# A planned instruction order replaced by another: new ranks and new engine choices for 1,088 steps of an RWKV6-plus-MLP kernel

## The chip, the cores and the metric

The kernel runs on one core of a Trainium2 chip. The metric is the time of one execution on the device in microseconds (us); smaller is better. The core has five engines that run side by side and wait for each other through semaphores: TensorE (PE; matmuls and, listed apart as PEld, their weight loads), VectorE (DVE), ScalarE (ACT), GpSimd (POOL) and SyncE (SP, which here issues nearly all DMA transfers). Each engine takes its instructions strictly in the order in which they were recorded. So an instruction that waits holds back everything recorded behind it on its engine, and the order in which independent work is recorded matters.

## The reference: what is computed

```python
def _attn_ref(r, k, v, w, u):                      # (4, 8, 768, 48) each, u (8, 48)
    for t in range(S):
        cur = np.einsum('bhd,bhe->bhde', u[None] * kt, vt)
        y[:, :, t] = np.einsum('bhd,bhde->bhe', rt, state + cur)
        state = wt[:, :, :, None] * state + np.einsum('bhd,bhe->bhde', kt, vt)

def _moe_ref(x, w_in, w_out):                      # x (3072, 384), w_in (384, 2048), w_out (2048, 384)
    h = x @ w_in
    g = np.maximum(0.01 * h, h)
    return g @ w_out
```

A linear-attention recurrence with per-channel decay w runs over 768 time steps for 4 batches of 8 heads; its output, 3072 rows of 384, goes through two dense layers with a leaky ReLU between them.

## The kernel before, in words

**Tiling.** The recurrence is cut into chunks of 128 time steps, 6 per batch, 24 in all, numbered in the order in which they are worked. The first two chunks of two batches are done as "pairs" (pair 0 is chunks 0 and 1, pair 1 chunks 2 and 3); chunks 4 to 23 are "singles", some of them merged in twos for their score matmuls. Within a chunk the recurrence is matmuls:

- SP loads w, k, r and v (L553 for pairs, L768 for singles), into a slot of the pool "in", which has ten.
- ScalarE takes the logarithm of w (lw, L567 and L778). TensorE sums it along time (L577, L784, with column totals at L591 and L787). VectorE makes ci (L796), ScalarE exponentials (L610, L810, L814; of the totals, a, L600 and L805), VectorE multiplies them onto r and k (rk, L468).
- rk is transposed to rkT by TensorE (L479, evacuated at L484 by VectorE or L486 by ScalarE) or, for 13 chunks, by a transposing DMA from SP (L831).
- TensorE makes scores (L691, L925), VectorE masks them (m, L703, L855); then TensorE makes the chunk's output from m and the cast v (vb) and from the carried state (L716, L723, L891, L896). The carried state is scaled by GpSimd (sb, L842), v is cast by GpSimd (vb, L518), the chunk's contribution to the state is made by TensorE (L650, L865) and added by VectorE (L880).
- The "bonus" of u: GpSimd multiplies k by u (ru, L498) and by r (L502), VectorE sums (dg, L506), GpSimd multiplies by v (L510; its result is named y in pairs, vs in singles). It is added by TensorE in pairs (L735) and by VectorE in singles (L541).
- The output y is transposed into xT by TensorE (L527, evacuated at L532 by VectorE or L534 by ScalarE) or, for 8 chunks, by DMA (L910).

The two dense layers are worked in 15 blocks of one or two chunks: "up" matmuls (L1087) into a bank of PSUM, the leaky ReLU by ScalarE (g, L1102), "down" matmuls (L1117), a copy to SBUF (o, L1128 or L1130), a store from SP (L1134). The last three blocks use a scheme with seven products instead of eight (sums at L1002, products at L1019, combinations at L1031 to L1040, stores at L1070). The weights w_in and w_out are loaded in parts by SP (L389, L394) and cast by whichever of GpSimd (L411), VectorE (L413) or ScalarE (L415) is chosen. L1159 are filler matmuls on zeros that stand in gaps of the first 24 us, to keep TensorE's clock up.

**What sets the order.** The program first lists 1,090 steps (`step(...)`): for each the engines that may do it with a planned duration on each, a priority number, the steps it depends on and the buffers it takes. Then `Plan.order` plays these through as a list scheduler: at each moment a free engine takes the ready step with the lowest priority number whose buffers are free. The order in which steps come out is the order in which their instructions are recorded, on every engine and in SP's DMA queue; buffers, too, are given out there. Two tables tune it. `RANK` has an offset for a step's priority number, `FORCE` fixes the engine of steps that several could do:

```python
        for i, x in RANK.items():
            plan.steps[i][2] = round(plan.steps[i][2] + x, 3)
        for i, e in FORCE.items():
            plan.steps[i][0] = {e: plan.steps[i][0][e]}
        order = plan.order(pools)
```

The recording loop behind it calls each step's function in that order, and puts filler matmuls ahead of a TensorE step where the plan has a gap.

Of the kernel before, what the change touches and what calls it, by code (L numbers as in the profile page):

```python
# [23 lines left out]
class Plan:  # L24
# [135 lines left out]
STORE = (0.45, 8, 0.9, 0.2)  # L160
TRK = (1.7, 64, 0.9, -0.6)
TY = (0.95, 24, 0.7, -0.6)
RANK = {0: 15.37, 1: 14.4, 2: 3.33, 3: 23.03, 5: 38.76, 6: 12.01, 7: -26.8, 8: -21.87, 9: -21.96, 10: -19.05,
# [63 lines left out]
FORCE = {24: "DVE", 27: "DVE", 30: "ACT", 31: "DVE", 47: "ACT", 59: "ACT", 62: "ACT", 80: "ACT", 86: "DVE",  # L227
    113: "DVE", 115: "ACT", 118: "DVE", 120: "ACT", 122: "ACT", 124: "DVE", 126: "POOL", 128: "ACT", 129:
    "POOL", 135: "POOL", 138: "DVE", 140: "POOL", 143: "ACT", 144: "POOL", 493: "DVE", 501: "ACT", 605: "DVE",
    613: "ACT", 905: "DVE", 911: "DVE", 933: "ACT", 953: "ACT", 967: "ACT", 1003: "ACT", 1031: "ACT", 1076:  # L230
    "ACT", 1081: "ACT"}


@with_exitstack
def kernel(
# [95 lines left out]
    with tc.manual_schedule():  # L331
# [810 lines left out]
        step({"PE": 0.0}, lambda e: None, 1000.0, deps=[up_first[2]], reads=[warm])  # L1142
# [51 lines left out]
```

## Time and profile before

| | |
|---|---|
| median of 3 runs | 181.74 us (180.81 to 182.94) |
| the profiled execution | 180.97 us, of which the span from first to last instruction is 179.3 us |
| TensorE clock granted in it | 0.997 of full speed |
| TensorE busy | 170.3 us of 179.3 |
| VectorE, ScalarE, GpSimd busy | 131.9, 116.5, 103.4 us |
| moved by DMA | 34.43 MB, mean 192 GB/s |

"Busy" is the time in which at least one instruction of the engine ran. The page cuts the span into 40 slices and gives the busy share of each in tenths. The timeline of an engine lists its instructions in order of time, equal neighbours merged: start, duration from the first's start to the last's end, engine, line, operation, tiles; in square brackets the idle time ahead and what ended it. As matmuls are pipelined, the listed end of one may lie behind the start of the next; starts are what is compared here.

### The profile page before, as it was taken

To read this page: it belongs to the slowest core of one execution; us is meant where nothing else is said; L and a number is where in the kernel's file an instruction comes from. 1 tells how busy PE (TensorE), PEld (TensorE's weight loads), DVE (VectorE), ACT (ScalarE), POOL (GpSimd) and SP (SyncE) were. 2 spreads that over 40 slices of the span, in tenths; PEclk is the share of its full clock that TensorE was granted. 3 is DMA by queue.
4 is the path that set the end of the run, shared out by engine and by line. 5 is a ranking of instruction groups with operands and counts; after the bars stand their busy time and mean duration, and the time that the engine had idled before them with its cause. 6 is when DMAs were issued, how large, how long until landed. Compare 5 with 4: busy or idle time off the path is not lost.

```text
span 179.3 us, 5364 instructions
## 1 busy us (share of the span) xinstructions
PE 170.3 (95%) x2102; PEld 133.8 (75%) x2105; DVE 131.9 (74%) x266; ACT 116.5 (65%) x259; POOL 103.4 (58%) x138
## 2 busy tenths in 40 slices
PE   7798899999989999999999999999999999999991
PEld 2555778867868688787688777777778798899991
DVE  7799664189769899459687659499787599777472
ACT  4679868855957688895379775176685487735620
POOL 5998532675697586878468855414996448110000
PEclk9999999999999999999999999999999999999998
DMA  6999999999999899999999999979799996813004
GB/s 150 261 284 317 371 378 358 185 195 201 227 185 203 170 223 143 182 208 184 200 199 194 220 178 229 208 151 140 146 205 140 195 214 139 184 24 115 0 22 154
DMA packets 116716, 34.43 MB, mean 192 GB/s; under 512 B 109138, under 2 KB 115923, under 8 KB 116691
## 3 DMA queue, kind: packets, MB, share of 16 engines
q1 hardware_dynamic: 116688, 34.09, 94.6%
q8 instruction: 16, 0.26, 0.7%
q14 instruction: 10, 0.07, 0.2%
q10 hardware_dynamic: 2, 0.00, 0.0%
HBM read 25.17 MB, written 4.72 MB: 167 GB/s over the span
## 4 chain that ended last, share of the span: by engine, by line
PE 57%; DMA 12%; POOL 8%; issue 7%; SPq 6%; DVE 4%; ACT 4%; DVEq 0%; POOLq 0%; ACTq 0%
PE ps L1087 26%; PE ps L1117 14%; DMA in<-in_v_dram 8%; PE ps L1019 6%; SPq L553 4%; DMA in<-in_k_dram 3%; PE ps L925 2%; POOL ru L498 2%; SPq L389 2%; DMA in<-in_r_dram 2%; ACT g L1102 2%; POOL ru L502 2%; POOL sb L842 1%; DVE o L1040 1%; PE ps L896 1%
## 5 line engine op out<-in xcount | busy, mean ns | idle before, releaser
L1087 PE MATMUL ps<-xT,w_in_b 128*128 128x256 bf16 (+1 forms) x720 | 73.2, 251 | 0.2 <-ACT xT L534 0.2
L1102 ACT ACTIVATE g<-ps 128x512 bf16<-128x512 f32 x96 | 56.5, 595 | 20.7 <-PE ps L1087 15.2
L1087 PEld LDWEIGHTS <-w_in_b 128*128 128x128 bf16 x720 | 57.5, 98 | 9.2 <-issue 0.7
L1117 PE MATMUL ps<-w_out_b,g 128*128 128x384 bf16 x288 | 56.0, 326 | 0.1
L1117 PEld LDWEIGHTS <-g 128*128 128x128 bf16 x288 | 25.7, 97 | 12.3 <-ACT g L1102 0.2
L498 POOL TENSOR_TENSOR ru<-in,ub 128x384 f32<-128x384 f32 x24 | 24.6, 1028 | 11.0 <-DMA in<-in_k_dram 10.8
L468 DVE TENSOR_TENSOR rk<-in,ps 128x384 bf16<-128x384 f32 x48 | 25.0, 549 | 7.4 <-ACT ps L810 4.2
L855 DVE TENSOR_TENSOR m<-ps,maskb 128x512 bf16<-128x512 f32 x40 | 25.4, 684 | 6.1 <-PE ps L925 5.1
L502 POOL TENSOR_TENSOR ru<-ru,in 128x384 f32<-128x384 f32 x24 | 24.3, 1018 | 2.7 <-DMA in<-in_r_dram 2.1
L842 POOL TENSOR_TENSOR sb<-s,a 128x384 bf16<-128x384 f32 x18 | 15.7, 873 | 8.9 <-ACT a L805 8.7
L510 POOL TENSOR_TENSOR vs<-in,dg 128x384 f32<-128x384 f32 x20 | 16.6, 828 | 7.4 <-DVE dg L506 4.9
L518 POOL CAST vb<-in 128x384 bf16<-128x384 f32 x24 | 12.0, 504 | 12.0 <-DMA in<-in_v_dram 12.0
L506 DVE TENSOR_REDUCE dg<-ru 128x8 f32<-128x384 f32 x24 | 13.1, 546 | 2.3 <-POOL ru L502 2.1
L796 DVE TENSOR_TENSOR ci<-ps,lw 128x384 f32<-128x384 f32 x20 | 11.1, 554 | 3.7 <-PE ps L784 1.7
L778 ACT ACTIVATE lw<-in 128x384 bf16<-128x384 f32 x20 | 10.4, 520 | 3.0 <-DMA in<-in_w_dram 3.0
L810 ACT ACTIVATE ps<-ps 128x384 f32<-128x384 f32 x20 | 9.5, 474 | 4.1 <-DVE ci L796 3.8
L541 DVE TENSOR_TENSOR y<-ps,vs 128x384 bf16<-128x384 f32 x20 | 11.1, 554 | 1.4 <-PE ps L896 0.6
L880 DVE TENSOR_TENSOR s<-ps,sb 128x384 f32<-128x384 f32 x14 | 7.7, 552 | 3.9 <-PE ps L865 1.4
L814 ACT ACTIVATE ps<-ci 128x384 f32<-128x384 f32 x20 | 9.8, 488 | 0.6 <-DVE ci L796 0.6
L805 ACT ACTIVATE a<-ps 64x4 f32<-64x4 f32 x36 | 6.0, 167 | 5.6 <-DVE ci L796 3.8
L534 ACT COPY xT<-ps 128x384 bf16<-128x384 bf16 x11 | 5.2, 478 | 6.9 <-PE ps L527 6.9
L1019 PEld LDWEIGHTS <-g 128*128 128x128 bf16 x96 | 8.0, 98 | 0.5 <-ACT g L1102 0.4
(105 smaller groups left out, 222.3 us busy)
## 6 DMA issues: line engine op xcount, KB each, us to landing
out_dram<-o SPq DMA_DIRECT2D x23, 192.0 KB, 3.2
in<-in_w_dram SPq DMA_DIRECT2D x20, 192.0 KB, 4.2
in<-in_k_dram SPq DMA_DIRECT2D x20, 192.0 KB, 4.2
in<-in_r_dram SPq DMA_DIRECT2D x20, 192.0 KB, 4.3
in<-in_v_dram SPq DMA_DIRECT2D x20, 192.0 KB, 4.3
in<-in_moe_w_out_dram SPq DMA_DIRECT2D x4, 768.0 KB, 12.1
in<-in_moe_w_in_dram SPq DMA_DIRECT2D x4, 384.0 KB, 7.0
in<-in_moe_w_in_dram SPq DMA_DIRECT2D x2, 768.0 KB, 9.2
```

Source lines behind the costliest of these rows:

```text
L468: (nc.gpsimd if e == "POOL" else nc.vector).tensor_tensor(out=o, in0=x, in1=i, op=ALU.mult)
L498: lambda e: nc.gpsimd.tensor_tensor(out=ru.t[:], in0=kv(), in1=ubv, op=ALU.mult),
L502: lambda e: nc.gpsimd.tensor_tensor(out=ru.t[:], in0=ru.t[:], in1=rv(), op=ALU.mult),
L506: lambda e: nc.vector.tensor_reduce(out=dg.t[:], in_=ru.t[:], axis=AX.X, op=ALU.add),
L510: lambda e: nc.gpsimd.tensor_tensor(out=vs.t[:], in0=vv(), in1=dg.t[:].unsqueeze(2).to_broadcast([128, H, D]), op=ALU.mult),
L518: {"POOL": 0.56}, lambda e: nc.gpsimd.tensor_copy(out=vb.t[:], in_=vv()),
L842: lambda e: nc.gpsimd.tensor_tensor(out=sb.t[:].rearrange("p g a d -> p (g a) d"), in0=s_in.t[:].rearrange("p g a d -> p (g a) d"), in1=a_ ...
L855: lambda e, par=par: nc.vector.tensor_tensor(out=m.t[:, par, :, :], in0=sc[par].t[:].rearrange("p (g t) -> p g t", g=NP), in1=maskb[:].uns ...
L1019: nc.tensor.matmul(o(), lhsT=x()[:, i, :], rhs=y()[:, i, :], start=fresh, stop=(stop and i == ii[-1]), skip_group_check=True)
L1087: nc.tensor.matmul(hp.t[:, a * N : (a + 1) * N], lhsT=w_in_b[:, t, (j + a) * 128 : (j + a + 1) * 128], rhs=xT[:, t, c0 : c0 + N], start=(a ...
L1102: lambda e, hp=hp, g=g, j=j, J=J, N=N: nc.scalar.activation(out=g.t[:, j : j + J, 0:N], in_=hp.t[:, 0 : J * N].rearrange("p (a n) -> p a n ...
L1117: nc.tensor.matmul(op.t[:, 0:DM], lhsT=g.t[:, j, off : off + 128], rhs=w_out_b[:, j, :], start=(j == 0), stop=(j == NJ - 1))
```

## The change

The change replaces the two tables and nothing else; no function is touched. Below it `RANK` gets offsets for all steps from 0 to 1087 (before: 0 to 144, 492 to 716 and 902 to 1087, with gaps), `FORCE` fixes the engine of 69 steps (before: 36). The new tables come from a search in which every operation of VectorE, ScalarE and GpSimd was lengthened at random. The first lines of each:

```diff
-RANK = {0: 15.37, 1: 14.4, 2: 3.33, 3: 23.03, 5: 38.76, 6: 12.01, 7: -26.8, 8: -21.87, 9: -21.96, 10: -19.05,
-    11: -14.59, 12: 18.77, 13: 18.75, 14: -2.55, 15: 18.27, 16: -16.59, 17: -21.47, 18: -19.49, 19: -20.48,
...
+RANK = {0: -59.43, 1: -52.42, 2: -98.27, 3: -101.28, 4: -69.43, 5: 951.62, 6: -68.29, 7: -162.82, 8: -162.92,
+    9: -101.74, 10: -20.83, 11: -89.42, 12: -137.74, 13: 931.61, 14: -77.73, 15: 931.11, 16: -90.39, 17:
...
-FORCE = {24: "DVE", 27: "DVE", 30: "ACT", 31: "DVE", 47: "ACT", 59: "ACT", 62: "ACT", 80: "ACT", 86: "DVE",
...
+FORCE = {4: "ACT", 24: "DVE", 27: "ACT", 30: "DVE", 33: "ACT", 47: "ACT", 57: "ACT", 59: "ACT", 60: "ACT", 62:
...
```

What comes out, by listing both programs' instructions on each engine:

| engine | steps before | steps after | mean shift in place | largest |
|---|---|---|---|---|
| TensorE | 320 | 320 | 3.2 | 22 |
| VectorE | 248 | 247 | 2.0 | 16 |
| ScalarE | 258 | 258 | 2.4 | 20 |
| GpSimd | 120 | 121 | 2.3 | 12 |
| SP (transfers) | 144 | 144 | 3.2 | 23 |

39 steps change their engine (weight casts, evacuations of rkT and xT, copies of o, two first states). Filler matmuls go from 36 to 41. In the first stage the changes that stand out are these:

- SP's queue: 1st part of w_in ahead of pair 1's k instead of behind it; then, behind pair 1's v, second quarter of w_out, first quarter of w_out, last quarter of w_in, third and fourth quarter of w_out (before: first quarter of w_out, last of w_in, second, fourth, third of w_out).
- GpSimd, pair 1: vb, vb, y, y (before: y, vb, vb, y).
- TensorE: eight groups of L1087 (of 0.65 us or a little more each) stand between pair 1's L735 and the first L1117 (before: five).

Later, SP loads some chunks' k or v ahead of an earlier chunk's r or v: chunk 7's w and k come before chunk 6's r and v; chunk 10's v goes from the 52nd to the 60th place in the queue. GpSimd's L498 for chunk 7 comes before chunk 6's vb, for chunk 10 before chunk 9's L498 and chunk 10's sb, for chunk 12 before the vb and the sb of chunk 11. The order of TensorE's last eleven steps stays as it was. All line numbers of the changed kernel are 73 higher behind the tables (L1087 becomes L1160, and so on).

More of the change, by code (lines that the diff above doesn't have):

```diff
@@ L162 @@
 TY = (0.95, 24, 0.7, -0.6)
-RANK = {0: 15.37, 1: 14.4, 2: 3.33, 3: 23.03, 5: 38.76, 6: 12.01, 7: -26.8, 8: -21.87, 9: -21.96, 10: -19.05,
[63 rows of a table removed]
-FORCE = {24: "DVE", 27: "DVE", 30: "ACT", 31: "DVE", 47: "ACT", 59: "ACT", 62: "ACT", 80: "ACT", 86: "DVE",
[L228 to L231, printed above, removed]
+RANK = {0: -59.43, 1: -52.42, 2: -98.27, 3: -101.28, 4: -69.43, 5: 951.62, 6: -68.29, 7: -162.82, 8: -162.92,
[133 rows of a table added]
+FORCE = {4: "ACT", 24: "DVE", 27: "ACT", 30: "DVE", 33: "ACT", 47: "ACT", 57: "ACT", 59: "ACT", 60: "ACT", 62:
+    "ACT", 80: "ACT", 83: "DVE", 86: "DVE", 89: "ACT", 103: "DVE", 113: "DVE", 115: "DVE", 116: "ACT", 120:
+    "ACT", 122: "POOL", 124: "POOL", 126: "ACT", 128: "ACT", 129: "POOL", 131: "POOL", 132: "ACT", 134: "DVE",
+    135: "POOL", 137: "DVE", 138: "DVE", 141: "POOL", 143: "DVE", 158: "DVE", 160: "ACT", 187: "ACT", 189:
+    "DVE", 198: "ACT", 202: "DVE", 240: "ACT", 262: "DVE", 278: "ACT", 280: "ACT", 309: "DVE", 311: "ACT",
+    325: "DVE", 384: "DVE", 422: "ACT", 436: "DVE", 493: "DVE", 613: "ACT", 737: "ACT", 771: "ACT", 785:
+    "ACT", 799: "ACT", 849: "ACT", 855: "ACT", 877: "DVE", 883: "ACT", 905: "ACT", 933: "ACT", 939: "DVE",
+    953: "ACT", 967: "ACT", 1003: "ACT", 1031: "DVE", 1034: "ACT", 1039: "ACT", 1076: "ACT", 1081: "ACT"}
 @with_exitstack
```

194 rows, old and new, of the table RANK are left out of this document.

## The prediction

> **What bounds the kernel now.** I read the page first, then the windows, then the timeline of TensorE around every hole, then the same stretch on the engine named as the releaser. The page:
>
> ```profile
> PE 170.3 (95%) x2102; PEld 133.8 (75%) x2105; DVE 131.9 (74%) x266; ACT 116.5 (65%) x259; POOL 103.4 (58%) x138
> PE   7798899999989999999999999999999999999991
> PEclk9999999999999999999999999999999999999998
> ```
>
> TensorE is the bound: busy 95%, at full clock (0.997 granted over the span), full in nearly every slice from the sixth to the last but one. A busy matmul may overlap the next, so I measure holes another way: from the start of one group of matmuls to the start of the next, less what the same group takes elsewhere when nothing waits (four L1117 0.65 us, twelve 128-column L1087 0.67, four L479 0.22, eight L1019 0.66). The timeline of TensorE at the largest hole after the start:
>
> ```profile
> 52.46 0.39 PE L479 MATMUL ps<-ident,rk 128*128 128x128 bf16 x4
> 53.45 0.33 PE L865 MATMUL ps<-vb,rk 128*128 128x96 bf16 x4 [0.60 <-POOL vb L518]
> ```
>
> 53.45 - 52.46 - 0.22 = 0.77 us. The same reckoning gives 0.38 at 62.0 (L1087 waits for ScalarE's xT copy, L534), 0.17 and 0.22 at 132, 0.27 at 149 (L1019 waits for the third of three g's in a row), 0.49 at 174.7 (L1019 waits for VectorE, L1040), and 0.26 in three small ones: **2.6 us from 23.6 us on**. Each group of scores (L925) also loses about 0.1 us before and after it (38.58 to 39.33 for four L1117 is 0.75, not 0.65), a dozen times; the change keeps these groups, so that stays.
>
> Before 23.6 us TensorE waits for pair 1 (the second batch's first two chunks). GpSimd's rows there, then TensorE's:
>
> ```profile
> 19.89 0.83 POOL L510 TENSOR_TENSOR y<-in,dg 128x384 bf16<-128x384 f32 x1 [2.53 <-DMA in<-in_v_dram]
> 20.66 0.95 POOL L518 CAST vb<-in 128x384 bf16<-128x384 f32 x2
> 21.57 0.83 POOL L510 TENSOR_TENSOR y<-in,dg 128x384 bf16<-128x384 f32 x1
> ...
> 21.66 0.47 PE L650 MATMUL ps<-vb,rk 64*128 64x96 bf16 x14 [0.23 <-POOL vb L518]
> ```
>
> The v load lands shortly before 19.89, GpSimd does one bonus multiply (y), then the two vb casts, and only then can L650 run: 0.69, 0.40 and 0.38 us of hole between 20.5 and 22.8. At the other end, L1019's last eight matmuls start at 175.16, the last store at 176.40, and the span ends at 179.3.
>
> So: from the L1087 at 23.62 to the end of the matmuls at 175.98 are 152.4 us, 2.6 of them holes. The set of steps left at that point is the same in the new order, so are their durations and the tail. The time can change only through (a) when that point comes, (b) the holes, (c) the tail.
>
> **The change part by part.** No arithmetic is added; all 320 TensorE steps keep their set and move by 3.2 places on average, at most 22. 39 steps change between VectorE, ScalarE and GpSimd (xT copies, rkT evacuations, weight casts, o copies), leaving 247, 258 and 121 steps against 248, 258 and 120: the loads move by under 1 us per engine, and none of the three is above 74%. Filler matmuls (L1159) go from 36 to 41, all ahead of 24 us; they stand where the planner saw gaps, and TensorE has 1.5 us of holes there, more than five of them (0.06 us for 128 columns, 0.22 for 512): nothing.
>
> (a) *The start.* GpSimd now does both vb casts (0.95) ahead of the first y multiply: L650 can start 0.8 us earlier (20.85). The final add of pair 1 (L735) needs both y's, which end at 22.4 as before, so it moves from 23.19 to about 22.5: -0.7. What is late next: chunk 4's first matmul (L784, at 35.36) has the same amount of TensorE work ahead of it and its w load still stands behind all weights in SP's queue. Its ScalarE logarithm ran at 34.56, 0.4 us before its k load (GpSimd waits until 34.93 for that). So most of the 0.7 is waited for again there. Bounds 0 and -0.7; I take **-0.3**.
>
> *Weights.* SP now fetches the second quarter of w_out, then the first, and the last quarter of w_in after both. The transfers landed at 24.99, 27.02, 29.11, 31.19 and 33.35 (rows of L411 and L413 that wait for them), so the one that moves comes 2.1 us later or earlier. The first L1117 needs the first quarter: landed 27.02, cast by 27.85; TensorE gets to it, after three groups of L1087 more than now (0.67 each) at 28.4. Covered by 0.6. The last quarter of w_in, 29.11, is cast by 30.0 and used at 31.0. Covered by 1.0; if the start gains nothing, by 0.7 more each.
>
> One cover is thinner than that. Where a GpSimd and a VectorE cast began together, one was long:
>
> ```profile
> 33.38 1.22 POOL L411 CAST w_out_b<-in 128x768 bf16<-128x768 f32 x1 [1.37 <-DMA in<-in_moe_w_out_dram]
> 33.35 0.56 DVE L413 CAST w_out_b<-in 128x768 bf16<-128x768 f32 x1 [3.68 <-DMA in<-in_moe_w_out_dram]
> ```
>
> against 0.83 alone: +0.39. Before has two such pairs (27.0, 33.4), the new order three. At 27.02 this would leave 0.2 of the 0.6. The Trainium skill (SBUF — State Buffer, section Who interferes with whom) says that such a VectorE copy locks GpSimd out for its whole length; by that the pair would cost 0.56, not 0.39, and the first L1117 would just be covered. The trace has the one cast lengthened, by less than that.
>
> (b) *The holes.* The 0.77 at 52.5: L865 waits for chunk 7's vb. On GpSimd that cast stood behind L498 (ru), which waited until 49.42 for chunk 7's k, and behind vs, sb and the second ru (0.82 + 0.83 + 0.99). Now one ru (1.00) stands between, 1.6 us less, and the k load goes out before chunk 6's r and v and before three stores. The hole goes: **-0.77** (0 if L498 waits longer than now).
> The 0.38 at 62.0: the copy moves from ScalarE (0.48, behind two a's that waited for ci) to VectorE (0.36, where masks and ci are queued): **-0.2**, between 0 and -0.38. Small ones: **-0.1** of 0.26.
> New: at 131 a cumulative sum (L784) follows the L1087 that allows its logarithm after 0.65 us of TensorE work, where it had 1.30; the one that now has 0.82 lost 0.17, so this one 0.17 + 0.17: **+0.3**. The 0.39 at 132 and 0.27 at 149 keep their distances. Three down groups come 1.00 to 1.10 us after the L1087 whose g they need (they had 1.30 to 7). At 149 a distance of 0.92 cost 0.27, so about 1.19 is needed when three g's queue, and 0.92 when none does: 0 to +0.4; **+0.2**.
> The rest: some 300 moves whose cover no row shows. Count of dependencies through another engine with under 0.3 us to spare in TensorE work: 19 before, 16 now; under 1 us: 64 and 74. It is no looser an order. Below by 0, above by as much as this order has, 2.6; nearer the low end, as two thirds of the present holes are priced already: **+0.5**.
>
> (c) *The tail.* One output copy (L1033, 0.35 in VectorE's chain of 173.20 to 175.1) goes to ScalarE, whose own next copy then ends the wait: bounds 0 and -0.35; **-0.1**.
>
> Sum: -0.3 - 0.77 - 0.2 - 0.1 + 0.3 + 0.2 + 0.5 - 0.1 = -0.5 us. The profiled execution took 180.97 (span 179.3 and 1.7 around it): 180.5. Its own time is 0.8 under the median of 181.74; against the median the same sum gives **181.2**.
>
> **Rivals.**
> 1. *As many holes, elsewhere.* The new waits equal those removed; only the start's -0.3 or nothing is left: 181.7. For it: the counts above. Against: the largest hole has a plain cause that is moved.
> 2. *The order has air where the old one had none.* All 2.6 of holes but the 0.39 + 0.27 kept go, with the start's 0.3 and 0.2 of the tail: -2.4, so 179.3. For it: most holes come from a step that was a little late, and that is what lengthening at random punishes. Against: the tight distances counted, and 0.3 at 131.
> 3. *Slower: GpSimd is held by L498.* L498 for chunks 7, 10 and 12 now stands ahead of a vb or sb that is needed sooner. It waited 10.8 us for k in 11 places, 0.98 each, where mostly nothing urgent stood behind. If the k loads land no earlier against GpSimd's place, three such waits reach L865 or the L891 that need vb and sb: +2.9 in place of the +0.5, and the -0.77 gone, which leaves -0.2 of the other terms: +2.7, so 184.4 uncovered; a quarter of it covered gives 183.7. It decides where a k lands over 0.5 us after GpSimd gets to it. Against: SP issues those k loads earlier.
> 4. *That it does nothing* can't be: the orders differ on all five queues.
>
> **How the numbers follow.** Forecast 0.35, rival 1 0.18, rival 2 0.21, rival 3 0.26. A change of under 1% (1.8 us) is about what a measurement here can't tell from none, so forecast and rival 1 are "same": faster 0.21, same 0.53, slower 0.26. The range goes from rival 2 to rival 3, with 0.3 to 0.5 for the bounds of the small terms: 179.0 to 184.2.
>
> **What would show it.** L650 of pair 1 at about 20.9 and chunk 4's L784 still near 35.2; no wait of L865 for vb near 52; a short wait of L784 near 131; the tail 3.3 us after the last matmul. A wait of L865 or L891 for GpSimd over 0.7 us, behind an L498 that waits for k, shows rival 3. I would be wrong if weights land in another rhythm, or if VectorE or ScalarE queues, of which I priced only what made a hole before, hold TensorE.

## The result, and the profile after

Beside each other on one chip the kernel before took 181.38 us (median of 20 executions) and the changed one 180.77 (20). The ratio is **0.9935, with a 95% interval of 0.9911 to 0.9959**, 1.2 us faster, when executions that lie over 1.5% above the fastest of their kernel are left out (five of these twenty of the changed kernel, 182.44 to 184.75, and one of the six of e12 below; with them the two medians are 0.6 us apart). Repeated on two other chips the ratio was 0.9917 [0.9890, 0.9944] and 0.9908 [0.9874, 0.9942], 1.5 and 1.7 us. The forecast said 0.5 us faster, under 1% and so "same": range and class hold, the gain by the ratios is 2.4 to 3.4 times as large. The profiled executions show less of it (180.97 us, span 179.3, against 180.35, span 178.6), since executions of one kernel spread over some 2 us and one profile is one of them.

The changed kernel's page:

```profile
PE 171.6 (96%) x2110; PEld 135.0 (76%) x2110; DVE 130.2 (73%) x265; ACT 116.1 (65%) x259; POOL 104.7 (59%) x139
PE   7898999999999999999999999999999999999992
PEclk9999999999999999999999999999999999999998
```

TensorE still bounds, at full clock. GpSimd's timeline in the start (start, duration, engine, line, tiles; in brackets the idle time ahead and its cause):

```profile
19.68 0.96 POOL L591 CAST vb<-in 128x384 bf16<-128x384 f32 x2 [1.55 <-DMA in<-in_v_dram]
20.60 1.61 POOL L583 TENSOR_TENSOR y<-in,dg 128x384 bf16<-128x384 f32 x2
```

Both vb casts now run ahead of both y's. TensorE's timeline (L723 is L650 of before, L808 is L735, L938 is L865, L552 is L479, L1190 is L1117):

```profile
21.21 0.51 PE L723 MATMUL ps<-vb,rk 64*128 64x96 bf16 x16
...
22.80 0.50 PE L808 MATMUL ps<-y,spread 64*128 64x384 bf16 x4
...
51.86 0.81 PE L1190 MATMUL ps<-w_out_b,g 128*128 128x384 bf16 x4
52.51 0.33 PE L938 MATMUL ps<-vb,rk 128*128 128x96 bf16 x4
52.68 0.39 PE L552 MATMUL ps<-ident,rk 128*128 128x128 bf16 x4
...
65.06 0.62 PE L552 MATMUL ps<-ident,rk 128*128 128x128 bf16 x8 [0.21 <-DVE rk L541]
...
127.61 0.83 PE L1160 MATMUL ps<-xT,w_in_b 128*128 128x128 bf16 x12 [0.32 <-DMA xT<-y]
...
156.18 0.40 PE L998 MATMUL ps<-rkT 48*128 48x128 bf16 x8 [0.25 <-DMA rkT<-rk]
...
174.82 0.82 PE L1092 MATMUL ps<-w_out_b,in 128*128 128x192 bf16 x8 [0.25 <-DVE o L1113]
```

The sums start at 21.21, and the state's matmul at 52 us follows its down group without a gap: the largest hole of before is gone. But there are new ones: transposes that wait for rk (hole 0.37 us, from start to start), up products that wait for xT's transposing DMA (0.48), scores that wait for rkT's (0.41). By the same reckoning as in the prediction, from 23 us on:

| profile | first sum (L784) of chunk 4 | holes 23-54 us | 54-115 | 115-170 | 170- | all | last matmul to end | span |
|---|---|---|---|---|---|---|---|---|
| before | 35.20 | 0.76 | 0.50 | 0.65 | 0.48 | 2.40 | 3.53 | 179.3 |
| before, repeated (e3) | 35.06 | 0.80 | 1.27 | 0.64 | 0.49 | 3.20 | 3.53 | 179.8 |
| after | 34.90 | 0.21 | 0.92 | 0.89 | 0.41 | 2.44 | 3.24 | 178.6 |
| after, repeated (e4) | 34.97 | 0.12 | 0.37 | 1.50 | 0.41 | 2.41 | 3.22 | 178.7 |
| after, third (e12) | 34.66 | 0.90 | 0.34 | 0.31 | 0.42 | 1.97 | 3.22 | 177.7 |

"Last matmul to end" counts from the start of the last matmul in the trace. Means of the two and the three: the start 0.29 earlier (35.13 to 34.84), holes 0.53 less (2.80 to 2.27), the end 0.30 shorter (3.53 to 3.23). That is 1.1 us, close to the difference of the mean spans (1.2, from 179.5 to 178.4) and to what the timed executions give. The first pair of profiles differs by 0.6, near the forecast, but by other pieces than forecast: 0.30 at the start, nothing in the holes, 0.28 at the end. So three pieces had to be tested: the start, the holes, the end.

### The profile page after: what moved, and what is told of

It reads as the page before. It is cut to its first block, busy times and chain, and to the rows that moved or that the text cites. A ratio compares the mean times of both kernels' runs of the same rounds, so it can differ in the third digit from the quotient of the medians.

```text
span 178.6 us, 5383 instructions
## 1 busy us (share of the span) xinstructions
PE 171.6 (96%) x2110; PEld 135.0 (76%) x2110; DVE 130.2 (73%) x265; ACT 116.1 (65%) x259; POOL 104.7 (59%) x139
## 4 chain that ended last, share of the span: by engine, by line
PE 58%; DMA 14%; SPq 11%; DVE 4%; POOL 4%; ACT 4%; issue 3%; POOLq 0%; DVEq 0%
PE ps L1160 23%; PE ps L1190 14%; SPq L841 10%; PE ps L1092 8%; DMA in<-in_k_dram 5%; DMA xT<-y 3%; DMA in<-in_v_dram 3%; DMA rkT<-rk 2%; POOL ru L571 2%; PE ps L998 2%; DMA in<-in_r_dram 2%; PE ps L552 1%; PE ps L969 1%; PE ps L1232 1%; PE ps L964 1%
## 5 line engine op out<-in xcount | busy, mean ns | idle before, releaser
L1160 PE MATMUL ps<-xT,w_in_b 128*128 128x256 bf16 (+1 forms) x720 | 72.2, 251 | 0.4 <-DMA xT<-y 0.3
L1175 ACT ACTIVATE g<-ps 128x512 bf16<-128x512 f32 x96 | 55.9, 595 | 24.5 <-PE ps L1160 21.3
L1160 PEld LDWEIGHTS <-w_in_b 128*128 128x128 bf16 x720 | 57.6, 98 | 8.5 <-issue 0.5
L1190 PE MATMUL ps<-w_out_b,g 128*128 128x384 bf16 x288 | 55.8, 326 | 0.0
L1190 PEld LDWEIGHTS <-g 128*128 128x128 bf16 x288 | 25.9, 98 | 12.4
L571 POOL TENSOR_TENSOR ru<-in,ub 128x384 f32<-128x384 f32 x24 | 23.9, 998 | 13.0 <-DMA in<-in_k_dram 10.6
L915 POOL TENSOR_TENSOR sb<-s,a 128x384 bf16<-128x384 f32 x18 | 15.2, 844 | 11.6 <-ACT a L878 11.5
L583 POOL TENSOR_TENSOR vs<-in,dg 128x384 f32<-128x384 f32 x20 | 17.6, 883 | 4.6 <-DVE dg L579 1.7
L1203 ACT COPY o<-ps 128x384 f32<-128x384 f32 x14 | 6.7, 478 | 5.8 <-PE ps L1190 5.8
L1232 PE MATMUL ps<-zeros 128*128 128x128 bf16 (+1 forms) x41 | 9.1, 337 | 1.3 <-DVE zeros L405 1.3
## 6 DMA issues: line engine op xcount, KB each, us to landing
in<-in_moe_w_out_dram SPq DMA_DIRECT2D x4, 768.0 KB, 10.6
```

Source lines behind the costliest of these rows:

```text
L571: lambda e: nc.gpsimd.tensor_tensor(out=ru.t[:], in0=kv(), in1=ubv, op=ALU.mult),
L583: lambda e: nc.gpsimd.tensor_tensor(out=vs.t[:], in0=vv(), in1=dg.t[:].unsqueeze(2).to_broadcast([128, H, D]), op=ALU.mult),
L915: lambda e: nc.gpsimd.tensor_tensor(out=sb.t[:].rearrange("p g a d -> p (g a) d"), in0=s_in.t[:].rearrange("p g a d -> p (g a) d"), in1=a_ ...
L1160: nc.tensor.matmul(hp.t[:, a * N : (a + 1) * N], lhsT=w_in_b[:, t, (j + a) * 128 : (j + a + 1) * 128], rhs=xT[:, t, c0 : c0 + N], start=(a ...
L1175: lambda e, hp=hp, g=g, j=j, J=J, N=N: nc.scalar.activation(out=g.t[:, j : j + J, 0:N], in_=hp.t[:, 0 : J * N].rearrange("p (a n) -> p a n ...
L1190: nc.tensor.matmul(op.t[:, 0:DM], lhsT=g.t[:, j, off : off + 128], rhs=w_out_b[:, j, :], start=(j == 0), stop=(j == NJ - 1))
```

## The experiments

Three theories. *Start*: the 0.3 of the vb casts and the 0.77 at 52 us are the gain. *Rest*: it is gained behind 54 us. *Whole*: a part of the order is worth nothing without the others. A fourth came up on the way: the 0.3 at the end is not a matter of order at all.

**Cuts of the order.** Six kernels have one order for the steps that the planner starts before some time, and the other behind:

```diff
-        order = plan.order(pools)
...
+        for item in ORDER.split():
+            i, e = int(item[:-1]), name[item[-1]]
...
+            plan.steps[i][1](e)
```

The list ORDER, which takes the place of the tables and of the planner's call, holds first the steps that the one order starts before a time T, then all others in the sequence of the other order; engines and filler matmuls are those of the order that a step comes from. In e1 and e2 (T = 35) buffers were handed out anew in the order of recording.

e1, new up to 35 us:

> The new order for every step that the new plan starts in its first 35 us, the old order behind it (same steps, same arithmetic). Theory A, the gain sits in the start: chunk 4's first cumulative sum on TensorE 0.3 us earlier than in the kernel before (34.9 against 35.2), and the time 0.3 us less (ratio 0.998) with the old holes at 52 and 62 back; 0.8 us less would mean that the start is worth more than the traces show. Theory B, the gain sits in how the rest of the order takes lateness: no more than 0.3 us, and the sister kernel has 0.6 to 0.9.

e2, new from 35 us:

> The old order for every step that the old plan starts in its first 35 us, the new order behind it. Theory A (the two orders have as many holes behind the start): within 0.3 us of the kernel before, ratio 0.998 to 1.002. Theory B (the new order has fewer or shorter holes over many executions, which one profile does not show): 0.6 to 0.9 us less, ratio 0.995 to 0.997. Either: chunk 4's first cumulative sum near 35.2, no wait of the state matmuls for a cast of v near 52.

e3 and e4, the two kernels unchanged:

> The kernel before, unchanged, for a second profile and as a measure of what the comparison can tell. Ratio 1.000 within 0.002. The hole at 52 (0.77 us) comes again if it belongs to the order; it moves or goes if it belongs to one execution.

> The changed kernel, unchanged, for a second profile. Ratio 0.9935 (0.991 to 0.996). The holes found in its first profile (0.37 at 64.6, 0.48 at 127.0, 0.41 at 155.7) come again if they belong to the order.

Measured, with the ratio to the kernel before on that chip (181.21): e1 183.28, **1.0175** [1.0124, 1.0225]; e2 181.05, **1.000** [0.9979, 1.0020]; e3 0.9996 [0.9972, 1.0019]; e4 0.9917. e1 and e2 say little of the cut: in front of the last products, where TensorE waits for VectorE's combinations, they have a hole of 1.66 and 1.32 us, where every other kernel has 0.41 to 0.49, and e1 has 2.99 us of holes up to 54 us besides (before: 0.76 and 0.80). With the buffers of the orders themselves, below, the hole in front of the last products is 0.41 to 0.49 again; but the place of the cut changed too, so that the new buffers alone are to blame is not shown. e3 and e4 answer what their texts ask. In e4 the three holes of the changed kernel came again (0.37, 0.69, 0.63). In e3 the wait of before at 52 us for the cast of v did not: TensorE waits 0.33 us at the next step there, for another load (shown in the part on why the prediction was right or wrong).

So the cuts were made again with each step's own buffers (renumbered where the two orders meet), at places where both orders hold the same steps but for none (21 us), two (54) or three on each side (115).

> The new order for every step planned in the first 54 us, with its engines, filler matmuls and buffers; behind that the old order with the old engines and buffers (renumbered at the seam so that no transfer waits for another buffer than in the old kernel; the two orders differ there by two steps). The whole change measured about -1.5 us between medians. Theory 'start': the vb casts ahead of the y multiply in pair 1 give 0.3 and the wait at 52 us that is gone gives up to 0.8, so -0.3 to -1.1 here, over half of the whole. Theory 'rest': what is gained is gained behind 54 us, by waits that vary from one execution to the next; then 0 to -0.3 here. Theory 'same as before' (everything hangs together, a part of the order alone is worth nothing): +0.5 or more.

> The other half: the old order for the first 54 us, the new one behind. Theory 'start': -0.4 or less gain. Theory 'rest': -1.2 to -1.5. The two halves should add up to about -1.5 if each part of the order is worth the same in either surrounding; if they add up to much less, the gain hangs on the whole.

> The new order for the steps planned in the first 21 us only (the two orders hold the same set of steps there): pair 1's vb casts ahead of its y multiplies on GpSimd, the first part of w_in ahead of pair 1's k, the other sequence of the weight transfers, 41 filler matmuls. Behind it the old order. By the prediction's term for the start: chunk 4's first cumulative sum 0.3 earlier (34.9 instead of 35.2) and the whole 0.3 faster, with the 0.3 to 0.8 at 52 us still there. Rival: the 0.3 is waited for again behind it, at the next load that TensorE needs: 0.

> The old order for the first 115 us, the new one behind. Between this and the new order from 54 us lies what 54 to 115 us are worth. By the traces of the two kernels: the waits at 132 and 149 us (0.3 to 0.4 and 0.27) go, waits for transposing DMAs come at 127 (0.48 to 0.69) and 155.7 (0.41 to 0.63), and the last products come 0.1 sooner: 0 in sum, between -0.4 and +0.4. If the gain of 1.5 is gained late, -0.8 or more.

| kernel | median us (before there: 182.09) | ratio | 95% interval | difference |
|---|---|---|---|---|
| e7, new up to 21 us | 181.74 | 1.0002 | 0.9972 to 1.0032 | 0 |
| e5, new up to 54 us | 182.15 | 1.0008 | 0.9981 to 1.0036 | +0.1 |
| e6, new from 54 us | 180.89 | 0.9933 | 0.9904 to 0.9961 | -1.2 |
| e8, new from 115 us | 181.44 | 0.9967 | 0.9939 to 0.9995 | -0.6 |

The differences are worked out from the ratios, whose intervals reach 0.5 us either way; e7's median alone is 0.35 under that of before. The halves add up to the whole of the other chips (+0.1 and -1.2, against 1.2 to 1.7), so "whole" falls, and "start" falls: **the first 54 us are worth nothing measurable, what is gained is gained behind them**, about half of it behind 115 us (-0.6, between the two cases of e8's text). In e5 chunk 4's sum came at 34.63, half a microsecond early, and the holes behind it were 1.00 up to 54 us and 2.32 from 54 to 115 (1.21 of them one wait for a transposing DMA at 81 us): in this profile what the start brings was waited for again. e7 is not a clean test of the start. TensorE's timeline:

```profile
25.80 1.34 PE L1127 MATMUL ps<-xT,w_in_b 128*128 128x128 bf16 x21
28.48 0.82 PE L1157 MATMUL ps<-w_out_b,g 128*128 128x384 bf16 x4 [1.35 <-DVE w_out_b L453]
```

and VectorE's:

```profile
27.23 1.20 DVE L453 CAST w_out_b<-in 128x768 bf16<-128x768 f32 x1 [1.79 <-DMA in<-in_moe_w_out_dram]
```

The new sequence of weights brings the first quarter of w_out 2 us later, but the old order behind 21 us has five groups of up products ahead of the first down group and not eight: a hole of 1.51 us. It puts chunk 4's sum at 36.42, 1.3 us later than in before and e3, and yet the last matmul comes only 0.3 to 0.8 us later than theirs and the median is the same: much of it was made up by waits behind it that grew shorter (e7 has none at 52 us).

**The end.** The time from the last matmul to the end was 3.22 to 3.24 us in e2, e4, e6 and the changed kernel, 3.53 to 3.59 in before, e1, e3, e5, e7 and e8. Not the tail's order decides (e8 has the new one) but a count. With the semaphore instructions, which the page leaves out, GpSimd's trace has 198 records in before and e3, 200 in e1, e7, e8, 202 in e5; and 208 in e6, 210 in e2, 211 in the changed kernel. In those with 198, GpSimd does nothing for 0.33 us after the fifth of the seven records with which it closes the program; with 200, for 0.32 to 0.34 after the third; with 202, for 0.36 after the first. That is **always between its 196th and 197th record**; the gaps between the other closing records are 0.03 to 0.07. With 208 or more the place lies ahead of the closing, where GpSimd has time to spare. So a test that leaves the order alone:

```diff
     xT = pool.tile([128, KT, NCH * L], BF16, name="xT")
+    pad = pool.tile([128, 1], F32, name="pad")
...
             plan.steps[i][1](plan.eng[i])
+        for _ in range(12):
+            nc.gpsimd.memset(pad[:], 0.0)
```

> The kernel before with twelve tiny memsets (128x1) on GpSimd behind its last step, at about 157 us, where GpSimd has nothing left to do. In the profiles so far the time from the last matmul's start to the end is 3.53 to 3.59 us wherever GpSimd has 198 to 202 records in the trace (the kernel before, its repeat, the new order up to 21, to 35 or to 54 us, the new order from 115 us) and 3.22 to 3.24 us wherever it has 208 to 211 (the changed kernel, its repeat, the new order from 35 or 54 us). Theory 'code': these 0.3 us hang on how many instructions GpSimd has, not on their order; then 3.24 here, and about 0.3 us less in all, with TensorE's order as before. Rival 'order': they come from the order of the steps between 54 and 115 us; then 3.53 here and no difference.

Measured: 179.59 us (9 executions, 179.41 to 180.18) against 181.07, **0.9926 [0.9903, 0.9950]**: 1.3 us less, not 0.3, and as fast as the changed kernel on that chip (179.51). The end is as "code" said: 3.24 us with 210 records. GpSimd's and VectorE's timelines of e9 have it:

```profile
155.95 1.81 POOL L1166 MEMSET pad<- 128x1 f32 x12
...
174.78 0.36 DVE L1041 TENSOR_TENSOR o<-ps,o 128x192 f32<-128x192 f32 x1 [0.65 <-PE ps L1020]
```

and VectorE's of before:

```profile
176.01 0.36 DVE L1040 TENSOR_TENSOR o<-ps,o 128x192 f32<-128x192 f32 x1 [0.65 <-PE ps L1019]
```

From the start of this last combination to the end are 2.96 us in e9 (span 177.74) and 3.25 in before (179.26). So instructions that do nothing bring the 0.3, with the order unchanged. The other 1.0 us came as a surprise, and it is in the holes: 1.49 us in all (0 up to 54, 0.37, 0.64, 0.48), against 2.40 and 3.20 in the same order. TensorE's timeline of e9 at the places where before lost 0.77 and 0.38 (lines are one higher):

```profile
52.43 0.33 PE L866 MATMUL ps<-vb,rk 128*128 128x96 bf16 x4
52.60 0.33 PE L785 MATMUL ps<-lw,trev 128*128 128x384 bf16 x1
...
61.54 1.69 PE L1088 MATMUL ps<-xT,w_in_b 128*128 128x256 bf16 x14 [0.20 <-ACT xT L535]
```

The waits that hang on loads are gone, those that hang on ScalarE or VectorE (61, 131, 148, 173 us) are there as before. What differs is the loads. The page's DMA rows (issues, size of each, median us to landing; and the queue's packets, MB, share of 16 engines), of e9:

```profile
q1 hardware_dynamic: 116688, 34.09, 89.1%
...
in<-in_k_dram SPq DMA_DIRECT2D x20, 192.0 KB, 3.7
```

of before:

```profile
q1 hardware_dynamic: 116688, 34.09, 94.6%
...
in<-in_k_dram SPq DMA_DIRECT2D x20, 192.0 KB, 4.2
```

The same packets take less time. The loads of w, k, r and v for single chunks are packets of 192 bytes; between 45 and 160 us one takes 15.8 ns on average in e9 and 93% of them take 15 ns, while in the thirteen other profiles it is 17.3 to 20.2 ns and 61 to 79%. Between 23 and 45 us it is 15.6 against 16.8 to 18.9. The 384-byte packets of the pairs' loads are not faster (28.1 against 27.7 to 28.2). The difference is there long before 156 us, so it can't come from the running of the memsets. The other thing that e9 has is the new tile: it was put ahead of the load buffers, and moves them and everything behind them by 32 bytes (the first from byte 64,672 of its partition to 64,704, from an odd multiple of 32 to a multiple of 64). That this shift makes the loads quicker is argued from there being no other change to the kernel that could act so early; no run had the tile without the memsets or the memsets without the tile, so it is not shown.

**Single waits of the old order.** Two steps of the kernel before are moved: the xT copy on ScalarE ahead of the two a's, and a down group ahead of the up products that wait for a transposing DMA at 89 us.

```diff
         order = plan.order(pools)
+        for i, ahead in ((262, 302), (853, 857)):
+            order.remove(i)
+            order.insert(order.index(ahead), i)
```

> The kernel before with two steps moved: on ScalarE the xT copy that TensorE waits for at 62 us goes ahead of the two exponentials of the totals (a); on TensorE one group of down products goes ahead of the up products that wait for a transposing DMA at 89 us. The wait at 62 was 0.37 us in all five profiles with the old order, that at 89 was 0, 0.64, 0.35, 1.16 us and (within another seam) 0. If the gain of the change behind 54 us is the sum of such waits that went, this gives -0.37 and about -0.4 on average: 0.6 to 0.8 us less between medians. Rival: what is saved there is waited for at the next late load, 0 to -0.2.

Measured: 180.82 against 181.07, **0.9995 [0.9972, 1.0018]**. TensorE's timeline:

```profile
61.30 0.82 PE L1117 MATMUL ps<-w_out_b,g 128*128 128x384 bf16 x4
61.96 1.25 PE L1087 MATMUL ps<-xT,w_in_b 128*128 128x256 bf16 x10
...
88.50 0.82 PE L1117 MATMUL ps<-w_out_b,g 128*128 128x384 bf16 x4
89.55 1.14 PE L1087 MATMUL ps<-xT,w_in_b 128*128 128x256 bf16 x9 [0.23 <-DMA xT<-y]
```

The hole at 62 is gone (61.96 - 61.30 is one down group, 0.65). At 89 the down group now stands in front and the wait comes behind it, 0.40. The time did not change, as the rival said. In this profile the wait for the transfer at 89 is 0.40 (before 0, e3 0.64), and a sum at 91 waits 0.23 for a logarithm behind it, where before and e3 wait for nothing. That these are what gave the 0.38 of 62 us back is argued from one profile.

**Single waits of the new order**, by four moves on TensorE:

```diff
         order = plan.order(pools)
+        for i, ahead in ((815, 310), (938, 955), (714, 685), (1015, 688)):
+            order.remove(i)
+            order.insert(order.index(ahead), i)
```

> The changed kernel with four moves on TensorE, one for each wait that came back in both of its profiles: at 64.5 us (0.37 and 0.37) a group of up products ahead of the transposes of rk; at 127 us (0.48 and 0.69) a group of down products ahead of the up products that wait for xT's transposing DMA; at 155.7 us (0.41 and 0.63) the chunk output ahead of the scores that wait for rkT's transposing DMA, and one group of up products ahead of the next chunk output. If these waits go and nothing follows: 1.2 to 1.7 us less than the changed kernel beside it. If each is half given back at the next wait for a load: 0.6 to 0.8. If the waits only move: 0.

> The changed kernel once more, on the chip on which the other three run: 1.2 to 1.5 us faster than the kernel before, as on the two other chips; waits of TensorE of 0.3 us and more at 64.5, 127 and 155.7 us again if they belong to the order, at other places if they come from transfers that vary.

Measured: e11 180.33, 0.9966 [0.9938, 0.9994]; e12, the changed kernel beside it, 179.51, **0.9908** (6 executions). The moves cost 0.8 us, though not beyond doubt: the intervals just touch. None of the three cases of e11's text foresaw a loss. TensorE in e11:

```profile
63.68 1.47 PE L1160 MATMUL ps<-xT,w_in_b 128*128 128x256 bf16 x12
64.99 0.61 PE L552 MATMUL ps<-ident,rk 128*128 128x128 bf16 x8
...
129.94 1.50 PE L1160 MATMUL ps<-xT,w_in_b 128*128 128x128 bf16 x24
132.02 0.32 PE L857 MATMUL ps<-lw,trev 128*128 128x384 bf16 x1 [0.57 <-ACT lw L851]
```

The waits at 64.5 and 127 us are gone, that at 156 is 0.15; in their place stand 0.74 at 131 us, 0.51 at 159.5 (in front of the products, for VectorE) and 0.55 at 88, 3.31 us of holes in all. e12 has the wait at 64.4 (0.34) and 126.5 (0.31) again, none at 155.7: the first two belong to the order, and the sizes of those for transfers vary from one execution to the next.

## Why the prediction was right or wrong

**That TensorE bounds, and that only start, holes and tail can move the time**: right; the three measured pieces (0.29, 0.53, 0.30) give 1.1 of the 1.2 us between the mean spans.

**Start, -0.3.** Measured -0.30 in the profile pair and -0.29 in the means. The two vb casts are the cause, as forecast, but the exact hit is luck, since two errors cancel. The first L650 starts at 21.21 in both kernels, as an up group ahead of it is still running (forecast 20.85); before, only two of its matmuls ran then and the rest at 21.66, now all run at once. So the final add came 0.4 earlier (22.80) and not 0.7 (22.5). Two filler matmuls more, a term put at nothing, take 0.12 of that: the up group behind starts 0.27 earlier. From there to chunk 4's sum are 11.58 us before and 11.55 after, so the 0.4 that was to be waited for again there was not. That wait shows only where the start is earlier still: in e12, whose up group starts at 22.80, the sum waits 0.30 for a logarithm that waited for w until 34.08. And "start" was taken as gained for good. The cut at 54 us says that it isn't: with the old order behind it, it buys nothing. Whether these 0.3 us survive to the end with the new order behind is not shown.

**Weights, nothing.** Right. Half of the first quarter is cast by GpSimd (27.00 to 27.83), the other by VectorE beside it, done at 28.24, and the eight groups of up products cover it (first down group at 29.00); e7, which takes three of them away, pays 1.51. That 28.24 is just 27.02 + 0.83 + 0.39 is luck: the 0.39 was read from a pair in which GpSimd came second. Here VectorE came second, and its cast, 0.55 alone, took 1.20, so 0.65 more.

**The 0.77 at 52.5, gone.** No profile of the changed kernel has a gap there. But the forecast named one of two causes. The wait for vb stands only in the profile of before. In e3, e6, e8 and e10, which have the same order there, GpSimd got its k earlier (L498 at 48.44 to 48.86, not 49.42), and the hole is one step later, at the sum L784, which waits for ScalarE's logarithm of a w that has just landed: 0.33, 0.82, 0.65 and 0.53. TensorE's timeline of e3:

```profile
52.94 0.33 PE L865 MATMUL ps<-vb,rk 128*128 128x96 bf16 x4
53.44 0.32 PE L784 MATMUL ps<-lw,trev 128*128 128x384 bf16 x1 [0.17 <-ACT lw L778]
```

ScalarE's of before:

```profile
52.82 0.52 ACT L778 ACTIVATE lw<-in 128x384 bf16<-128x384 f32 x1 [1.82 <-DMA in<-in_w_dram]
```

There the logarithm ends at 53.34, so an earlier vb alone would have let the sum start at some 53.4 instead of 53.61: an estimate of 0.2, not 0.77. In the new order the logarithm runs 0.9 us earlier (51.87), and a transpose and a down group stand ahead of the sum (L857, at 53.55), so it waits for neither. e7, which comes there a microsecond later, and e9, with faster loads, have neither wait. And the new order has a wait at 42 us (0.12 to 0.34), for rk and so for a k load, that I had not listed.

**The 0.38 at 62, -0.2.** It went wholly, as the copy on VectorE is early enough. The hole at 64.5, 0.34 to 0.37 in three of three profiles, took its place.

**New at 131, +0.3.** 0.09 in the profile after. The distance was measured from the wrong step. ScalarE's timeline there:

```profile
131.05 0.47 ACT L883 ACTIVATE ps<-ps 128x384 f32<-128x384 f32 x1
131.55 0.52 ACT L851 ACTIVATE lw<-in 128x384 bf16<-128x384 f32 x1
```

The logarithm follows the exponentials of the chunk before without a pause, and these hang on that chunk's sum at 129.14, not on an up group. From that sum to the one at 132.13 TensorE has work that just covers ScalarE's chain. e11 moves a down group (0.65) out of this stretch: the two sums stay 2.99 us apart (129.03 and 132.02), and the wait is 0.74. The 0.27 at 149, which I had kept, didn't come in any profile of the changed kernel.

**The rest, +0.5.** This is the term that was mis-sized, with the ones above that share its sum: all holes together I had at -0.1; the profiles give -0.5 on average (2.80 to 2.27), between -1.2 and +0.04 by pair, so with two and three profiles even its size is uncertain. What I missed is that the old order's holes vary: behind 54 us, where its row of before has 1.63 us, e3 has 2.40, e7 2.12 and e5 3.5. My 2.6 was a low draw, and the new order was measured against it. What I could not see in one profile, either, were the waits for transposing DMAs at 127 and 155.7.

**Tail, -0.1.** The hole in front of the last product shrank by 0.07, as forecast. Four times as much came from where I had called the tail the same: the 0.3 us between GpSimd's 196th and 197th record. I had forecast the time behind the last matmul as unchanged (3.3 us from the last group's end), and named nothing that could change it.

**The rivals.** "As many holes elsewhere" describes the profile pair (2.40 and 2.44) and is wrong on the means; "air where the old order had none" (-2.4) was right in its sign and measured at half to two thirds of its size, but the order has new waits of its own, at 42, 64.5, 127 and 155.7 us; GpSimd held by L498 did not come: its wait for k is 10.6 us in 11 places, as before (10.8), and nothing behind it holds TensorE by 0.7.

What stays open: how much of the -0.9 behind 54 us that is not code (e6's 1.2 less 0.3) each stretch brings. In the profiles of the two whole kernels it is 0.5 of holes, but e6's own has no fewer behind 54 us (1.98) than the old order there (1.63 and 2.40), and e8's -0.6, without the code, is more than its profile explains (holes behind 115 us 0.92 against 1.1). So where the gain lies is shown by the cuts, but for the part that is not code the waits that bring it are not. And whether the 32 bytes add to the new order's gain wasn't tried.

## What to carry to other kernels

A wait of the bounding engine that is taken away alone need not make the kernel faster: in e10 the time stayed, and in e11 it rose, with new waits for two other engines and a transfer. In one profile a hole has the cause that came last; look whether another stands right behind it before pricing it in full. Loads that came faster took away all waits for loads at once (in e9's profile). Read the stretch after the last arithmetic as carefully as the rest, since it may change with the number of instructions on an idle engine. In an experiment put an added tile behind all others, so that it moves no buffer, and take three profiles before trusting a difference of a microsecond.

## What the runs showed of the hardware that was not expected

- **A pause of 0.32 to 0.36 us at a fixed place of GpSimd's program**, after its 196th record, seen in all seven profiles in which that place falls into the closing; in the seven in which it comes earlier, the gap there is 0.3 us at most and the closing has none. The page's DMA part shows code that arrives while the kernel runs (26 packets on two instruction queues, 0.33 MB). The Trainium skill (Runtime: NRT & Kernel Launch, section Instruction fetch mechanics) has the instruction memory refilled block by block, with the cost of a crossing mostly hidden; here, if it is such a crossing, it is not hidden once the program is at its end. That it is one is not shown.
- **Loads that take less time**: 15.8 ns for a 192-byte packet instead of 17.3 to 20.2, and 3.7 us for a k load to land instead of 4.0 to 4.8, in e9, the one kernel whose load buffers start at multiples of 64 bytes. That this is the cause is not shown.
- **The last sixteenth of a transfer comes late while the weights are loaded.** A transfer reports its landing in 16 parts; from 18 to 23 us the last comes 1.0 to 1.5 us behind the fifteenth in all fourteen profiles. In the transfers of weights behind that (up to 34 us) it is two or more of the 16 that come late, and the parts of one spread over 1.6 to 2.2 us.
